# FFT convolution and spectral mixing on one core: a fourth PSUM slot for the transforms that run alone, and a later start of the first x loads

## The chip, the cores and the metric

The kernel runs on 1 core of a Trainium2 chip. The metric is the device time of one execution in microseconds (us); lower is better. Before the change it is 498.45 us, the median of 3 runs (497.08 to 500.85). PE is TensorE's matmul unit, DVE is VectorE, ACT is ScalarE, POOL is GpSimd; SP issues DMAs.

## The reference

Two layers over 8 sequences of 5696 steps and 128 channels, a long convolution and then a spectral mixing of 64 modes:

```python
def _attn_ref(x, h):                       # x (8, 5696, 128), h (5696, 128)
    Xf = np.fft.rfft(x, n=2 * S, axis=1)
    Hf = np.fft.rfft(h, n=2 * S, axis=0)
    return np.fft.irfft(Xf * Hf[None], n=2 * S, axis=1)[:, :S, :]

def _moe_ref(x, w_r, w_i, w_ch):           # w_r, w_i (64, 128, 128), w_ch (128, 128)
    X = np.fft.rfft(x, axis=1)
    Y = np.zeros_like(X)
    Xr, Xi = np.real(X[:, :64]), np.imag(X[:, :64])
    Y[:, :64] = (Xr @ w_r - Xi @ w_i) + 1j * (Xr @ w_i + Xi @ w_r)   # per mode
    u = x + np.fft.irfft(Y, n=S, axis=1)
    return u + np.maximum(u @ w_ch, 0.0)
```

## The kernel before, in words

**Transforms as matmuls.** The transform length 11392 is split as 89 x 128. A first transform (45 rows of a sequence against a small constant matrix) and a second one (a 128 x 128 constant per frequency, with the twiddles in it) make the spectrum. The second transform's constants are M: `m_sb[0]` is the real part, `m_sb[1]` the imaginary part, `m_sb[2]` the negative of the imaginary part, which DVE makes on the chip (L359). M is loaded in six pieces: three chunks of 15 frequencies each, for each chunk the real and then the imaginary part (L316 to L319).

**Stages.** They run in this order:

1. h, first transform: 16 tiles of 16 small matmuls (loop at L346, tile `Ah`), and then the three negations of M, one per chunk, on DVE.
2. h, second transform: 12 tiles of up to 16 matmuls (`h_tile`, from L368; reads `Ah` and M, writes `Hs`). Tiles 0 to 3 need M's first chunk, tiles 3 to 7 the second, tiles 7 to 11 the third.
3. x, first transform of the first pair of sequences: 32 tiles of 4 matmuls (`a_tile(j, True)`, L388; reads `Xin`, writes `As`). "Alone" means that nothing else is on PE meanwhile.
4. Four groups, each a pair of sequences: 27 ticks (`tick`, L409) do the second transform of two frequencies at a time, the product with `Hs` on DVE, a first inverse step that goes to a DRAM scratch, and the first 64 modes, which add up in PSUM bank 7 over the whole group. The next pair's first transform runs beside the last four ticks (16 tiles, 4 a tick) and then alone (16 tiles, L522). Ahead of those 16, `modes_out` (L476) copies bank 7 into `XM`; behind them, `modes_turn` (L479) transposes `XM` through bank 6.
5. Mixing of the modes, and the output stage (`u_tile`, `o_tile`).

**Slots.** PSUM has 8 banks. A tile takes two neighbouring banks, and `tile2` (L285) turns over three slots: banks 0-1, 2-3, 4-5. Banks 6 (`TB`) and 7 (`MB`) are kept for the modes. A matmul that starts a tile waits until the copy out of that slot's last tile is done. Those copies (`evac`, L264) alternate between ACT and DVE; in the alone tiles of x, 9 of 16 go to ACT and 7 to DVE (L331). The output stage has a counter of its own over four slots.

**Order.** Every engine executes its list in program order; a recorder (`R.add`) works out the semaphore waits from the tokens that are read and written. `after=` adds waits by hand. L281 is the line of the helper that records every matmul, L272, L274 and L275 those of the copies out of PSUM, L278 that of every DMA. DMAs are issued from two queues, each in program order:

- SP: small constants, then M's six pieces (they wait for h's first half), then the identity, `FQ`, `WV`, and, with the ticks, `Gs` (constants of the modes, three ticks ahead, seven of them in the first 40 us), the writes to scratch and the output.
- POOL: h in three pieces, then the first pair of x in six (two halves and a tail per sequence; L320; they wait for both halves of h), then `w_ch`, then the next pairs of x.

Of the kernel before, what the change touches and what calls it, by code (L numbers as in the profile page):

```python
# [4 lines left out]
P = 128  # L5
# [118 lines left out]
def bass_long_conv_fft__then__afno_spectral_mix_kernel(nc, x, h, moe_w_r, moe_w_i, moe_w_ch, out):  # L124
# [48 lines left out]
    def const(name, a):  # L173
        return nc.inline_tensor(np.ascontiguousarray(a.astype(np.float16)), name=name)

    KW = NQ * P
    c_m = const("cM", np.stack([mat.real, mat.imag], axis=1).reshape(P, -1))
# [15 lines left out]
    def at(name, cols, dt, off):  # L193
        return nc.alloc_sbuf_tensor_at(name, [P, cols], dt, offset=off)
# [9 lines left out]
    m_sb = [at(f"M{i}", KW, F16, a_m + i * KW * 2) for i in range(3)]  # L204
# [41 lines left out]
    def ap(t, row, p0, n, off, dims):  # L246
        return bass.AP(t, p0 * row + off, [[row, n]] + [list(d) for d in dims])
# [4 lines left out]
    def pv(bank, off, dims, p0=0, n=P):  # L252
        return bass.AP(ps, p0 * 4096 + bank * 512 + off, [[4096, n]] + [list(d) for d in dims])
# [5 lines left out]
    def bank(i):  # L259
        return ("bank", i)  # L260
# [16 lines left out]
    def dma(eng, dst, src, ring, reads=(), writes=(), after=()):  # L277
        return R.add(eng, lambda h_: h_.dma_start(dst, src), reads, writes, ring=ring, after=after)  # L278

    def mm(o, l, r, st, sp, reads, writes):  # L280
        return R.add("tensor", lambda h_: h_.matmul(o, l, r, start=st, stop=sp), reads, writes)  # L281

    slot3 = [0]

    def tile2():  # L285
        slot3[0] = (slot3[0] + 1) % 3
        return 2 * slot3[0]

    TB, MB = 6, 7

# [8 lines left out]
    def x_pieces(g_):  # L299
        for b in range(2):  # L300
            p0, off = b * NQ, x.offset + (2 * g_ + b) * S * D
            for c in range(2):
                yield (x_sb[p0:p0 + NQ - 1, c * half:(c + 1) * half],
                       bass.AP(x.tensor, off + c * half, [[P * D, NQ - 1], [1, half]]), ("xin", b, c))
            yield (x_sb[p0 + NQ - 1:p0 + NQ, 0:TAIL * D],
                   bass.AP(x.tensor, off + (NQ - 1) * P * D, [[TAIL * D, 1], [1, TAIL * D]]), ("xin", b, 2))

    h_loads = [dma("gpsimd", h_in[64 * c:64 * c + NQ - 1, :],
                   bass.AP(h.tensor, h.offset + c * half, [[P * D, NQ - 1], [1, half]]), "x", (), [("hin", c)])
               for c in range(2)]  # L310
# [2 lines left out]
                       "x", (), [("hin", 2)]))  # L313
    NCH = 3
    CH = NQ // NCH * P
    for c in range(NCH):  # L316
        for i in range(2):
            dma("sync", m_sb[i][:, c * CH:(c + 1) * CH], bass.AP(c_m, i * KW + c * CH, [[2 * KW, P], [1, CH]]), "c",
                (), [("m", i, c)], after=h_loads[:1])  # L319
    for dst, src, tok in x_pieces(0):  # L320
        dma("gpsimd", dst, src, "x", (), [tok], after=h_loads[:2])
    dma("sync", wi_sb[:, P:2 * P], c_i.ap(), "c", (), [("i16",)])
    dma("sync", fq_sb[:, :], c_fq.ap(), "c", (), [("fq",)])
    dma("sync", wv_sb[:, :], c_w.ap(), "c", (), [("wv",)])
# [4 lines left out]

    def a_tile(j, alone):  # L330
        eng = ("scalar" if 9 * j % 16 < 9 else "vector") if alone else None  # L331
        t = tile2()
        for i in range(4):
            mm(pv(t + i // 2, (i % 2) * 256, [[1, 256]]),
               ap(x_sb, P * D, 0, 2 * NQ, 4 * j + i, [[D, P]]), f1_sb[0:2 * NQ, :], True, True,
               XT_, [bank(t + i // 2)])
        evac(bass.AP(a_sb, 4 * j, [[2 * AW, P], [P, 180], [2, 2], [1, 2]]),
             pv(t, 0, [[1, 180], [512, 2], [256, 2]]),
             [bank(t), bank(t + 1)], [("as", j)], 1.0 / 64, eng)
# [3 lines left out]

    HT = [("hin", c) for c in range(3)] + [("hz",), ("fh",)]
    for j in range(16):
        t = tile2()  # L346
        for i in range(8):
            d = 8 * j + i
            for c in range(2):
                h_done = mm(pv(t + i // 4, (i % 4) * 90, [[1, 90]], 64 * c, 64),  # L350
                            ap(h_in, 64 * D, 64 * c, NQ, d, [[D, 64]]), fh_sb[64 * c:64 * c + NQ, :],
                            True, True, HT, [bank(t + i // 4)])
        evac(bass.AP(ah_sb, 8 * j, [[AW, P], [P, 90], [4, 2], [1, 4]]),
             pv(t, 0, [[1, 90], [512, 2], [90, 4]]),
             [bank(t), bank(t + 1)], [("ah", j)], 1.0 / 64)
    AHT = [("ah", j) for j in range(16)]
    for c in range(NCH):
        cs = slice(c * CH, (c + 1) * CH)
        R.add("vector", lambda e, cs=cs: e.tensor_scalar_mul(m_sb[2][:, cs], m_sb[1][:, cs], -1.0),  # L359
              [("m", 1, c)], [("m", 2, c)])  # L360

    def m_tok(k):
        return [("m", i, k * P // CH) for i in range(3)]

# [1 line left out]
    FORWARD = ((0, 0, 2), (1, 1, 0))  # L366

    def h_tile(j):  # L368
        t = tile2()
        ks = list(range(4 * j, min(4 * j + 4, NQ)))  # L370
        for i, k in enumerate(ks):
            b, o = t + i // 2, (i % 2) * 256
            re = bass.AP(ah_sb, (2 * k) * P, [[AW, P], [1, P]])
            im = bass.AP(ah_sb, (2 * k + 1) * P, [[AW, P], [1, P]])
            kc = slice(k * P, k * P + P)
            for half_, l0, l1 in FORWARD:
                o2 = o + half_ * P
                mm(pv(b, o2, [[1, P]]), m_sb[l0][:, kc], re, True, False, AHT + m_tok(k), [bank(b)])
                mm(pv(b, o2, [[1, P]]), m_sb[l1][:, kc], im, False, True, AHT + m_tok(k), [bank(b)])
        n = len(ks)  # L380
        evac(bass.AP(h_sb, 4 * j * P, [[2 * KW, P], [P, n], [KW, 2], [1, P]]),
             pv(t, 0, [[256, n], [P, 2], [1, P]]),
             [bank(t), bank(t + 1)], [("h", j)], 8.0)
# [119 lines left out]
    for g_ in range(NP):  # L503
        more = list(x_pieces(g_ + 1)) if g_ + 1 < NP else []
        todo_a = list(range(32)) if more else []
        for t in range(NT + LM):
            done = tick(g_, t)
            if t in X_AT and more:
                dst, src, tok = more.pop(0)
# [48 lines left out]
    m_done += [R.readers[tok][-1] for tok in HST]  # L558
    n_ev = [0]

    slot4 = [0]

    def tile4():
        slot4[0] = (slot4[0] + 1) % 4
        return 2 * slot4[0]

    def u_tile(i, b):
        g_, c = divmod(i, 8)
        t = tile4()
        for hb in range(2):  # L570
            o = pv(t + hb, 0, [[1, 360]])
            mm(o, c_sb[:, (2 * g_ + b) * P:(2 * g_ + b + 1) * P],
               ib_sb[:, (c * 16 + hb * 8) * NQ:(c * 16 + hb * 8 + 8) * NQ], True, False,
               [("c", g_ // 2), ("ib",)], [bank(t + hb)])
            for pl in range(8):
                o2 = (hb * 8 + pl) * 256 + b * P
                f0 = step * (c * 16 + hb * 8 + pl) % NA
                mm(pv(t + hb, pl * NQ, [[1, NQ]]), zt[i % NC][0:2 * NQ, o2:o2 + P], fq_sb[0:2 * NQ, f0:f0 + NQ],
                   False, pl == 7, [("zt", i % NC), ("fq",)], [bank(t + hb)])
        ub = (g_ % 2) * 2 + b  # L580
        n_ev[0] += 1
        evac(bass.AP(u_sb[ub], c * 16, [[KW, P], [P, NQ], [8, 2], [1, 8]]),
             pv(t, 0, [[1, NQ], [512, 2], [NQ, 8]]), [bank(t), bank(t + 1)],
             [("u", ub, c)], after=m_done, eng="scalar" if n_ev[0] % 8 in (0, 2, 3, 5, 7) else "vector")
# [3 lines left out]
    def o_tile(g_, b, r4):  # L588
        ub = (g_ % 2) * 2 + b
        bb = 2 * g_ + b  # L590
        t = tile4()
        i = n_o[0]
        n_o[0] += 1
        full = r4 < 11
        n, rows = (4, P) if full else (1, TAIL)
        rd = [("u", ub, c) for c in range(8)] + [("wch",), ("i16",)]
        for j in range(n):
            lh = bass.AP(u_sb[ub], 4 * r4 + j, [[KW, P], [44, P]]) if full else u_sb[ub][:, 44 * P:44 * P + TAIL]
            mm(pv(t + j // 2, (j % 2) * 256, [[1, 256]], 0, rows), lh, wi_sb[:, :], True, True, rd, [bank(t + j // 2)])
        bk = [bank(t), bank(t + 1)] if full else [bank(t)]  # L600
        rs, os_ = r_sb[i % NR], o_sb[i % NO]
        rv = bass.AP(rs, 0, [[512, rows], [P, n], [1, P]])
        ov = bass.AP(os_, 0, [[512, rows], [P, n], [1, P]])
        src_r, src_u = pv(t, 0, [[256, n], [1, P]], 0, rows), pv(t, P, [[256, n], [1, P]], 0, rows)
        R.add("scalar", lambda e: e.activation(rv, src_r, RELU), bk, [("r", i % NR)], after=[mixed])  # L605
        R.add("vector", lambda e: e.tensor_tensor(ov, src_u, rv, ADD), bk + [("r", i % NR)], [("o", i % NO)], after=[mixed])  # L606
        if full:
            dst = bass.AP(out.tensor, out.offset + bb * S * D + 4 * r4 * D, [[44 * D, P], [1, 4 * D]])
            src = o_sb[i % NO][:, :]
        else:  # L610
            dst = bass.AP(out.tensor, out.offset + bb * S * D + 44 * P * D, [[D, TAIL], [1, D]])
            src = o_sb[i % NO][0:TAIL, 0:P]
        dma("sync", dst, src, "o", [("o", i % NO)])
# [46 lines left out]
```

## Time and profile before

| | |
|---|---|
| time, median of 3 runs | 498.45 us |
| the profiled execution's own time | 496.65 us |
| its span, first to last instruction | 494.9 us |
| mean granted TensorE clock | 0.941 |
| PE busy | 422.2 us (85%) |
| DVE busy / ACT busy | 333.3 / 333.2 us (67% each) |
| h, first transform on PE | 16.5 to 31.5 us |
| h, second transform on PE | 33.3 to 50.7 us |
| x, first transform alone on PE | 51.0 to 71.5 us |
| the alone tiles of the next three pairs | from 133.2, 205.3 and 277.3 us, some 10 us each |

How to read it: times are from the span's start. A group "PE ps L281" is a matmul into PSUM. In the chain of work, each line is a start, a duration, and the work that the end of the program was waiting for then. In the lists of waits, the columns are the time waited in total, how often, and the longest. "PEclk" is the share of the full TensorE clock that was granted in a stretch.

### The profile page before, as it was taken

What the parts mean: (1) busy time and instruction counts of PE and PEld (TensorE: products, weight loads), DVE (VectorE), ACT (ScalarE), POOL (GpSimd) and SP (SyncE); (2) the same over time, 40 slices, a digit from 0 to 9 for tenths busy, and PEclk for the clock granted to TensorE, in tenths of its full rate; (3) what the DMA queues carried; (4) which work ended last, traced back from release to release, by engine and by line L of the source; (5) the groups of instructions that cost most, each with busy time, mean ns of one, the idle gap of its engine ahead of it and who ended that gap; (6) DMA issues with size and microseconds to landing.
All of it is one profiled execution on the core that took longest, in us unless ns stands there. A gap on an engine that the chain in (4) does not pass through costs nothing.

```text
span 494.9 us, 10143 instructions
## 1 busy us (share of the span) xinstructions
PE 422.2 (85%) x4188; PEld 333.7 (67%) x4188; DVE 333.3 (67%) x568; ACT 333.2 (67%) x416; POOL 41.2 (8%) x72
## 2 busy tenths in 40 slices
PE   0686998999989999979999979998598549597994
PEld 0686885777976777967777957776477427475873
DVE  0234759898669888869887679883137327465786
ACT  1233777988877988668988868984157426375795
POOL 1200000010100010100110010001031001010000
PEclk9998999999999999999999999999599858888998
DMA  8994008999909999919999369668789999999789
GB/s 129 282 169 118 1 0 141 250 235 250 191 19 155 264 259 227 180 21 188 272 222 251 89 158 274 183 164 228 239 213 257 282 309 360 313 350 320 293 296 341
DMA packets 97572, 105.05 MB, mean 212 GB/s; under 512 B 22924, under 2 KB 81692, under 8 KB 93724
## 3 DMA queue, kind: packets, MB, share of 16 engines
q1 hardware_dynamic: 75846, 63.47, 42.5%
q0 software_dynamic: 21680, 40.95, 41.2%
q8 instruction: 33, 0.54, 0.5%
q14 instruction: 13, 0.10, 0.1%
HBM read 74.82 MB, written 46.92 MB: 246 GB/s over the span
## 4 chain that ended last, share of the span: by engine, by line
PE 59%; DMA 25%; ACT 7%; DVE 6%; issue 1%; SPq 1%; DVEq 0%; ACTq 0%; POOLq 0%
PE ps L281 59%; DMA out_dram<-O 12%; DMA M<-cM 6%; DMA IBs<-cIB 4%; ACT R L605 3%; DMA zscr<-Zs 2%; DMA Hin<-in_h_dram 2%; ACT Xs L272 2%; DVE Pb L435 2%; DVE Xs L440 2%; DVE O L606 1%; DVE Xs L473 1%; ACT Zs L271 1%; ACT As L272 1%; SPq L278 1%
## 5 line engine op out<-in xcount | busy, mean ns | idle before, releaser
L272 ACT ACTIVATE Xs<-ps 128x1024 f16<-128x1024 f32 (+1 forms) x92 | 91.2, 1007 | 19.2 <-PE ps L281 19.2
L271 ACT CAST Zs<-ps 128x1024 f16<-128x1024 f32 (+1 forms) x92 | 93.4, 1017 | 12.5 <-PE ps L281 10.2
L281 PE MATMUL ps<-Xs,WV 128*128 128x512 f16 (+1 forms) x368 | 92.9, 375 | 7.7 <-DVE Xs L473 7.4
L281 PE MATMUL ps<-As,M 128*128 128x256 f16 x720 | 91.7, 273 | 3.4 <-ACT As L272 3.4
L606 DVE TENSOR_TENSOR O<-ps,R 128x512 f32<-128x512 f32 x96 | 59.3, 652 | 45.6 <-DMA out_dram<-O 27.9
L281 PE MATMUL ps<-F,Xin 90*128 90x256 f16 x512 | 80.1, 307 | 1.1 <-ACT Hs L272 0.3
L281 PEld LDWEIGHTS ps<-As,M 128*128 128x128 f16 x720 | 70.2, 98 | 12.9 <-DVE As L275 3.0
L435 DVE TENSOR_TENSOR Pb<-Xs,Hs 128x1024 f16<-128x1024 f16 (+1 forms) x92 | 62.4, 678 | 23.1 <-ACT Xs L272 22.9
L281 PEld LDWEIGHTS ps<-F,Xin 90*128 90x128 f16 x512 | 72.9, 232 | 7.4 <-DVE As L275 2.1
L473 DVE TENSOR_TENSOR Xs<-Xs,Pb 128x512 f16<-128x512 f16 (+1 forms) x184 | 77.3, 422 | 0.1
L275 DVE TENSOR_SCALAR As<-ps 128x720 f16<-128x720 f32 x59 | 58.8, 997 | 25.6 <-PE ps L281 24.8
L605 ACT ACTIVATE R<-ps 128x512 f32<-128x512 f32 x96 | 52.2, 573 | 32.7 <-PE ps L281 32.3
L272 ACT ACTIVATE As<-ps 128x720 f16<-128x720 f32 x69 | 60.8, 892 | 18.0 <-PE ps L281 17.9
L281 PE MATMUL ps<-WI,UT 128*128 128x256 f16 x360 | 58.6, 301 | 5.8 <-DVE O L606 5.6
L440 DVE TENSOR_TENSOR Xs<-Xs,Hs 128x1024 f16<-128x1024 f16 (+1 forms) x92 | 61.9, 672 | 0.1
L281 PE MATMUL ps<-IBs,C 128*128 128x360 f16 x128 | 44.7, 349 | 17.7 <-DVE O L606 16.5
L281 PEld LDWEIGHTS ps<-Xs,WV 128*128 128x128 f16 x368 | 35.0, 98 | 33.6 <-DVE Xs L473 10.9
L281 PE MATMUL ps<-Zs,Gs 128*128 128x256 f16 x360 | 54.3, 273 | 0.2 <-ACT Zs L271 0.2
L281 PEld LDWEIGHTS ps<-FQ,ZT 90*128 90x128 f16 x1024 | 45.0, 101 | 12.3 <-issue 3.5
L281 PE MATMUL ps<-FQ,ZT 90*128 90x45 f16 x1024 | 50.0, 189 | 1.6 <-issue 1.6
L281 PEld LDWEIGHTS ps<-Zs,Gs 128*128 128x128 f16 x360 | 35.0, 98 | 22.8 <-ACT Zs L271 1.6
L281 PEld LDWEIGHTS ps<-WI,UT 128*128 128x128 f16 x360 | 40.9, 154 | 12.5 <-DVE O L606 9.4
(41 smaller groups left out, 232.8 us busy)
## 6 DMA issues: line engine op xcount, KB each, us to landing
ZT<-zscr POOLq DMA_DIRECT2D x32, 720.0 KB, 10.3
zscr<-Zs SPq DMA_DIRECT2D x88, 256.0 KB, 5.9
out_dram<-O SPq DMA_DIRECT2D x88, 256.0 KB, 10.3
Gs<-cG SPq DMA_DIRECT2D x88, 128.0 KB, 5.8
Xin<-in_x_dram POOLq DMA_DIRECT2D x16, 704.0 KB, 8.3
M<-cM SPq DMA_DIRECT2D x6, 480.0 KB, 8.8
W<-in_moe_w_r_dram POOLq DMA_DIRECT2D x4, 512.0 KB, 10.2
W<-in_moe_w_i_dram POOLq DMA_DIRECT2D x4, 512.0 KB, 8.0
```

Source lines behind the costliest of these rows:

```text
L271: return R.add(e, lambda h_: h_.copy(dst, src), reads, writes, after=after)
L272: return R.add(e, lambda h_: h_.activation(dst, src, COPY, scale=scale), reads, writes, after=after)
L275: return R.add(e, lambda h_: h_.tensor_scalar_mul(dst, src, scale), reads, writes, after=after)
L278: return R.add(eng, lambda h_: h_.dma_start(dst, src), reads, writes, ring=ring, after=after)
L281: return R.add("tensor", lambda h_: h_.matmul(o, l, r, start=st, stop=sp), reads, writes)
L435: R.add("vector", lambda e: e.tensor_tensor(pbv, xv, hv[1], MULT), [tx] + HST, [tp], after=[h_done])
L440: R.add("vector", lambda e: e.tensor_tensor(xv, xv, hv[0], MULT), [tx], [tx])
L473: R.add("vector", lambda e: e.tensor_tensor(a, a, b, ADD if part else SUB), [("xs", s % NX), ("pb", s % NB_)], [("xs", s % NX), ("y", s % ...
L605: R.add("scalar", lambda e: e.activation(rv, src_r, RELU), bk, [("r", i % NR)], after=[mixed])
L606: R.add("vector", lambda e: e.tensor_tensor(ov, src_u, rv, ADD), bk + [("r", i % NR)], [("o", i % NO)], after=[mixed])
```

## The change

1. The counter of the slots takes their number. The first and second transforms of h and the alone tiles of x turn over four slots, banks 6 and 7 with them; tiles inside the ticks and beside them keep three. There is one counter now for all stages, the output stage too.
2. The first pair's x loads wait for h's second half and for the fourth piece of M (second chunk, imaginary part), where they waited for h's two halves.

```diff
-    slot3 = [0]
-
-    def tile2():
-        slot3[0] = (slot3[0] + 1) % 3
-        return 2 * slot3[0]
+    slot = [0]
+
+    def tile2(slots=3):
+        slot[0] = (slot[0] + 1) % slots
+        return 2 * slot[0]
...
+    m_loads = []
     for c in range(NCH):
         for i in range(2):
-            dma("sync", m_sb[i][:, c * CH:(c + 1) * CH], bass.AP(c_m, i * KW + c * CH, [[2 * KW, P], [1, CH]]), "c",
-                (), [("m", i, c)], after=h_loads[:1])
+            m_loads.append(dma("sync", m_sb[i][:, c * CH:(c + 1) * CH], bass.AP(c_m, i * KW + c * CH, [[2 * KW, P], [1, CH]]), "c",
+                (), [("m", i, c)], after=h_loads[:1]))
     for dst, src, tok in x_pieces(0):
-        dma("gpsimd", dst, src, "x", (), [tok], after=h_loads[:2])
+        dma("gpsimd", dst, src, "x", (), [tok], after=[h_loads[1], m_loads[3]])
...
     def a_tile(j, alone):
         eng = ("scalar" if 9 * j % 16 < 9 else "vector") if alone else None
-        t = tile2()
+        t = tile2(4 if alone else 3)
...
     for j in range(16):
-        t = tile2()
+        t = tile2(4)
...
     def h_tile(j):
-        t = tile2()
+        t = tile2(4)
...
-    slot4 = [0]
-
-    def tile4():
-        slot4[0] = (slot4[0] + 1) % 4
-        return 2 * slot4[0]
-
     def u_tile(i, b):
         g_, c = divmod(i, 8)
-        t = tile4()
+        t = tile2(4)
...
     def o_tile(g_, b, r4):
...
-        t = tile4()
+        t = tile2(4)
```

## The prediction

> **What bounds the kernel now**
>
> I read the page first, then the chain of work in order of time, then the waits and the timeline of its first 75 us, and last the timeline around the three later stretches of alone tiles.
>
> ```profile
> span 494.9 us, 10143 instructions
> ...
> PE   0686998999989999979999979998598549597994
> ...
> DMA  8994008999909999919999369668789999999789
> ...
> PE 59%; DMA 25%; ACT 7%; DVE 6%; issue 1%; SPq 1%; DVEq 0%; ACTq 0%; POOLq 0%
> ```
>
> One slice is 12.4 us. PE is the bound up to about 340 us, and time taken from PE's path there is taken from the end. Two stretches look soft: slices 2 to 4, where DMA is full too, and the stretches of alone tiles. The chain says what the first one is:
>
> ```profile
> 12.68 27.99 DMA M<-cM
> 40.69 0.66 DVE M L359
> 41.34 1.15 DVE Hs L275
> 42.54 8.07 PE ps L281 x112
> 50.62 1.38 ACT Hs L272
> 52.05 8.62 PE ps L281 x56
> ```
>
> The last piece of M, issued at 12.7, lands at 40.7; the negation waits for it; the copy of an `Hs` tile waits behind the negation on DVE; and PE waits for that tile's slot. The timeline shows the same from the engines' side (start, duration, engine, instructions, idle before):
>
> ```profile
> 33.27 5.42 PE L281 MATMUL ps<-Ah,M 128*128 128x128 f16 x64 [1.57 <-DVE M L359]
> ...
> 40.69 0.66 DVE L359 TENSOR_SCALAR M<-M 128x1920 f16<-128x1920 f16 x1 [6.90 <-DMA M<-cM]
> 41.26 2.35 DVE L275 TENSOR_SCALAR Hs<-ps 128x1024 f16<-128x1024 f32 x2
> 42.53 8.10 PEld L281 LDWEIGHTS ps<-Ah,M 128*128 128x128 f16 x116 [4.02 <-DVE Hs L275]
> 42.54 8.28 PE L281 MATMUL ps<-Ah,M 128*128 128x128 f16 x116 [3.85 <-DVE Hs L275]
> ```
>
> PE does 64 matmuls, four tiles, and stands still for 3.85 us. The clock pays again: the busy times by stretch have it at half speed in part of what follows (last columns: granted clock, DMA share, GB/s).
>
> ```profile
> 40.00:45.00 5.00, 2.46 (x33) 2.47 (x34) 2.92 (x3) 1.02 (x1) 0.00 (x0) 0.86 0.62 190
> 45.00:50.00 5.00, 5.00 (x75) 5.00 (x73) 2.72 (x3) 2.05 (x2) 0.00 (x0) 0.79 0.00 0
> ```
>
> In the matmuls' own records the starts are 107 ns apart from 33.3 to 36.8, 56 ns from there to the stall, 56 ns again for 1.1 us after it, 107 ns from 43.7 to 47.0, and 56 ns to the end of the stage at 50.65.
>
> **Why M is late.** The landing records give M's first four pieces at 17.1, 18.3, 19.5 and 20.75, one each 1.2 us, and the last two at 33.5 and 40.7. The x loads are issued from 16.58; their first packets move at 20.35, and then 16 KB packets of x (1.23 to 2.3 us each) share the engines with the rest of M. The last x lands at 42.3, the last of the `Gs` behind it at 45.3.
>
> **The alone tiles.** Undelayed, a tile of four matmuls takes PE 0.51 us (0.50 to 0.53, by the starts of those beside the ticks). In the alone stretch 30 tiles from 52.05 to 70.73 take 0.623 each: nearly every tile waits for its slot, and the first matmul of a waiting tile takes 0.24 us to the next, not 0.12 to 0.15. The copies meanwhile:
>
> ```profile
> 57.01 1.62 ACT L272 ACTIVATE As<-ps 128x720 f16<-128x720 f32 x2 [0.25 <-PE ps L281]
> 58.23 1.10 DVE L275 TENSOR_SCALAR As<-ps 128x720 f16<-128x720 f32 x1 [0.88 <-PE ps L281]
> 58.85 0.77 ACT L272 ACTIVATE As<-ps 128x720 f16<-128x720 f32 x1 [0.21 <-PE ps L281]
> ...
> 133.55 0.54 ACT L272 ACTIVATE XM<-ps 128x256 f16<-128x256 f32 x1
> ...
> 205.85 0.84 DVE L275 TENSOR_SCALAR XM<-ps 128x256 f16<-128x256 f32 x1
> ```
>
> (The last two are from the later stretches.) A copy takes 0.77 on ACT and 0.91 on DVE where it is undisturbed; where one of each overlaps, one of them takes 0.97 to 1.06 or 1.10 to 1.25. Both engines still wait for PE between copies, and PE for them: neither is full, so the three slots set the pace.
>
> **The change part by part**
>
> *x waits for M's fourth piece.* The wait ends at 20.75, not 16.5, so POOL issues x 4.2 us later. Behind x on POOL stands `w_ch` only, needed in the output stage; the next POOL instruction is at 75.9. SP's queue keeps its order. At 20.75 M has two pieces left, due at 21.9 and 23.1 at 1.2 us each. x's first packet follows its issue by 1.2 us (issue of 75.9) to 3.8 us (issue of 16.58), so comes at 22.0 to 24.5, when an engine has at most one piece's eight packets of M left. Before, the slowest engine needed 20.3 us for some 17 packets of M after x had come, 1.2 each; eight take at most 9.7, that is until 31.7. The third negation is due on DVE at 33.8, behind the `Ah` copies and two negations. Between 22 and 31.7 it makes no difference: the 6.9 us wait on DVE and the 3.85 on PE go. PE then runs through: 33 matmuls at 107 ns from 33.27 to 36.8, 147 at 56 ns, 8.2 us, end 45.0 instead of 50.65. The copies (ACT 1.02, DVE 1.23 for two tiles of 0.89) keep up. **Gain 5.65**, of it 3.85 the stall and most of the rest the half clock behind it. If the clock drops anyway, the gain is 3.85.
>
> *Is x there at 45.0?* It landed at 42.3 and starts 4.2 later: at worst 46.5. The other bound: an engine has 11 to 12 packets of x, 14.7 us at 1.23, from 22.0: 36.7, if nothing else moves. Between them: no transfer is added, and all of this traffic was done at 45.3; the engines have M to move until x comes, so x should not end after that. I take 42 to 44, and cost 0; bounds 0 and 1.5 (plus 1.7, half of a 3.4 us stretch at half clock, if the wait brings the clock down).
>
> *Four slots, h.* The first transform has PE at 107 ns a pair throughout, 0.89 per tile, against copies of 0.77 and 0.91 on alternate engines: no slot binds, 0. In the second one no slot binds once M is there, 0. At the entry to x, PE waits 0.36 us for DVE and 0.42 for ACT copies of `Hs` to free slots; a fourth slot covers both: **0.8**.
>
> *Four slots, the first 32 alone tiles.* With three, a slot's round (PE 0.66 to the end of the last matmul, start of the copy 0.04, copy 0.77 to 1.25, restart 0.06) is 1.5 to 2.0 us, 0.5 to 0.67 a tile, as seen. With four it is 0.38 to 0.5, below PE's 0.51. Next in line are the copies: of 16 tiles ACT has 9, at 0.81 to 1.03 with the turn, 0.46 to 0.58 a tile; DVE 7, at 0.95 to 1.18, 0.42 to 0.52. The pace lies between 0.51 (PE) and 0.62 (more overlap eats it all). I take 0.55, since PE's floor is 0.51 and overlapping copies, which will be the rule, put ACT above it: 30 x (0.623 - 0.55) = **2.2**, bounds 0 and 3.4.
>
> The Trainium skill, "PSUM — Partial Sum Buffer", Specifications (TRN2), says that ScalarE and VectorE read PSUM side by side at full bandwidth so long as they keep to different banks. These copies are in different banks and the rows above still stretch. By the page the pace would be PE's 0.51 and the sum 1.2 us better in these 32 tiles.
>
> *The later alone tiles, 3 x 16.* The same 0.07 a tile: 3.4. Against it a new wait: the fourth slot holds bank 7, which `modes_out` must have copied, and bank 6, which `modes_turn` needs. The counter, followed through the program, stands at 0 ahead of the ticks, so the fourth slot is the first alone tile of the first group, the second of the second, the third of the third. `XM` is copied by 134.09 and PE began that first tile at 133.15: 1.0 lost, with the other tiles and the next ticks behind it on PE. In the second group 206.69 against 205.98: 0.8. In the third 278.29 against 278.54: nothing. `modes_turn` waits at most for the last copy but one, while the next tick waits for the last: 0. Together 3.4 - 1.8 = **1.6**, bounds -1.8 and 3 x 16 x 0.11 - 1.8 = 3.5.
>
> The Trainium skill also has a case that speaks against this half of the change: in "TensorE: Matmul & The Clock Gate", HAM oscillation, a kernel that had been kept dense gained almost nothing from double-buffered PSUM (126.6 to 125.5 us). There the slots were not what PE waited for; here the 0.24 us first matmuls say that they are. By that case the sum would be 5.65 alone, less the new waits.
>
> *One counter.* The output stage begins on banks 4-5 instead of 2-3; its first tile needs the mixed modes either way: 0.
>
> *Sum.* 5.65 + 0.8 + 2.2 + 1.6 = 10.2 us. All of it lies ahead of 290 us, where PE is the chain; the tail moves as it stands. 496.65 - 10.2 = 486.4 for the profiled execution; the median of the runs shown is 1.8 above that execution, so 488.2.
>
> **The rivals**
>
> - *x becomes the wait.* x lands at up to 46.5 and PE stands still for 1.5, with 1.7 of half clock: 488.2 + 3.2 = 491.4. For it: x starts 4.2 later with a margin of 2.7. Against it: much of M is out of its way.
> - *The copies are the bound.* The pace stays at 0.62; 2.2 and 3.4 go: 493.8. For it: copies already stretch by 0.2 to 0.3 where they overlap. Against it: both engines wait for PE at 0.2 to 0.9 a time.
> - *M is late all the same,* behind x packets on one engine, past 38.5. A fifth tile is done ahead of the stall (16 x 0.056 = 0.9), and 5.65 shrinks to that: 492.9. Against it: eight packets are left at most.
> - *Slower: x lands so late that it eats everything.* The place is PE's first alone tile. The gains are gone when x lands at 45.0 + 10.2 = 55.2, and it is slower by over 1% from 60.2. That takes 12 packets from 24.5 at 3.0 us each; the slowest seen were 2.3 (then it lands at 52.1 and the time is 488.2 + 7.1 + 1.7 = 497.0).
>
> **How the numbers follow**
>
> My forecast has 0.68, x late 0.12, copies 0.11, M late 0.05, slower 0.04. The predicted time is the first's, 488.2. Its own range, with the bounds 0 and 3.4, -1.8 and 3.5, is 485 to 493; x late and most of the copies' case lie inside or just above. The range is 484.0 to 493.8: what is left out is the slower case, half of M late with more than one mishap, and a gain beyond all bounds, some 1.5 in 10. About 1%, 5.0 us, is what a measurement of this kernel can tell from no change, so faster means below 493.5: the forecast, x late, half of M late and a third of the copies' case, 0.85. Same 0.11, slower 0.04.
>
> **What would show it**
>
> M's last piece lands by 32 and DVE has no wait for it; the second transform of h runs from 33.3 to 45 without a pause and without a drop of the clock after 36.8; the last x lands before 45 (if not, PE shows a wait for a DMA of `Xin`); the alone tiles come at 0.55 and end on PE at about 62.5, not 71.5; PE waits 1.0 for the copy of `XM` on ACT in the first group and 0.8 for that on DVE in the second. The prediction is wrong if the third negation still waits, if x lands after 46.5, or if the alone tiles keep 0.62.

## The result and the profile after

The changed kernel takes 483.39 us (median of 4 runs, 481.19 to 484.3) against 498.84 (497.08 to 500.85): 15.4 us less, a ratio of 0.9683 with a 95% interval of 0.9633 to 0.9733. The forecast was faster, 488.2, in a range of 484.0 to 493.8. The direction held and both halves of the change paid, but the gain that was forecast, 10.2 us, was too small by a third, and the time lies 0.6 us below the range. The profiled execution took 481.19, with a span of 479.4; that of before 496.65 and 494.9, so the two profiles stand to each other as the medians do. One run of experiment 3 below (497.02 us) was in a slower state, and its median is given without it.

The page after; the rows are those shown of before, slices of 12.0 us:

```profile
span 479.4 us, 10143 instructions
...
PE   0689979999979999989999989996899369597994
...
DMA  7994049999749999769899298759699999999779
...
PE 56%; DMA 26%; ACT 7%; DVE 7%; issue 1%; POOL 1%; SPq 0%; DVEq 0%; ACTq 0%; POOLq 0%
```

The chain of work in its first 65 us (start, duration, what):

```profile
11.94 8.92 DMA M<-cM
21.14 2.51 POOL Xin L278 x5
23.65 21.39 DMA Xin<-in_x_dram
45.13 16.64 PE ps L281 x128
61.79 0.78 ACT As L272
62.62 1.06 PE ps L281 x8
```

The 28 us of M are gone from it. A transfer of x stands in their place, which ends at 45.0; then 128 matmuls follow each other without a wait, where before they were cut into pieces of 4 to 56. The timeline of the same stretch (start, duration, engine, instructions, idle before):

```profile
31.79 1.79 DVE L360 TENSOR_SCALAR M<-M 128x1920 f16<-128x1920 f16 x3
...
32.50 11.52 PE L281 MATMUL ps<-Ah,M 128*128 128x128 f16 x180 [1.58 <-DVE M L360]
...
45.13 16.63 PE L281 MATMUL ps<-F,Xin 90*128 90x256 f16 x128 [1.10 <-DMA Xin<-in_x_dram]
```

The three negations stand in a row, PE does all 180 matmuls of h's second transform in one run, and the first alone tile waits 1.1 us for x. In the landing records M's six pieces come at 17.2, 18.4, 19.6, 20.9, 22.1 and 23.4. Busy time by stretch (the last three columns are the granted clock, the DMA share and GB/s):

```profile
35.00:40.00 5.00, 5.00 (x90) 5.00 (x88) 3.08 (x3) 2.50 (x3) 0.00 (x0) 1.00 0.91 193
40.00:45.00 5.00, 4.02 (x73) 3.85 (x69) 3.38 (x4) 3.07 (x3) 0.00 (x0) 1.00 0.32 58
45.00:50.00 5.00, 4.87 (x38) 4.90 (x39) 3.23 (x4) 3.47 (x5) 0.00 (x0) 1.00 0.02 3
```

No second stretch at half clock. Where the 15.5 us of span came from, by the starts on PE in both profiles:

| stretch | before | after | gain | forecast |
|---|---|---|---|---|
| start to the first alone tile | 51.01 | 45.13 | 5.9 | 6.0 |
| first alone tile to the first tick | 21.36 | 17.49 | 3.9 | 2.6 |
| first group (ticks, then 16 alone tiles) | 71.81 | 70.64 | 1.2 | 1.6 for the three groups |
| second group | 72.24 | 70.82 | 1.4 | (see above) |
| third group | 71.96 | 70.26 | 1.7 | (see above) |
| last group's first tick to the end | 206.48 | 205.03 | 1.45 | 0 |

### The profile page after: what moved, and what is told of

Its sections match the earlier page's. It is cut to its first block, busy times and chain, and to the rows that moved or that the text cites. A ratio compares the mean times of both kernels' runs of the same rounds, so it can differ in the third digit from the quotient of the medians.

```text
span 479.4 us, 10143 instructions
## 1 busy us (share of the span) xinstructions
PE 411.6 (86%) x4188; PEld 326.9 (68%) x4188; DVE 329.9 (69%) x568; ACT 330.1 (69%) x416; POOL 41.5 (9%) x72
## 3 DMA queue, kind: packets, MB, share of 16 engines
q0 software_dynamic: 21680, 40.95, 42.3%
## 4 chain that ended last, share of the span: by engine, by line
PE 56%; DMA 26%; ACT 7%; DVE 7%; issue 1%; POOL 1%; SPq 0%; DVEq 0%; ACTq 0%; POOLq 0%
PE ps L281 56%; DMA out_dram<-O 12%; DMA Xin<-in_x_dram 4%; DMA IBs<-cIB 4%; ACT R L600 3%; DMA Hin<-in_h_dram 2%; DMA M<-cM 2%; DMA zscr<-Zs 2%; ACT Xs L272 2%; DVE Pb L436 2%; DVE Xs L441 2%; DVE O L601 2%; ACT Zs L271 1%; DVE Xs L474 1%; ACT As L272 1%
## 5 line engine op out<-in xcount | busy, mean ns | idle before, releaser
L281 PE MATMUL ps<-F,Xin 90*128 90x256 f16 x512 | 71.7, 295 | 2.2 <-DMA Xin<-in_x_dram 1.1
L281 PEld LDWEIGHTS ps<-F,Xin 90*128 90x128 f16 x512 | 68.2, 225 | 4.9 <-ACT Hs L272 1.2
L275 DVE TENSOR_SCALAR As<-ps 128x720 f16<-128x720 f32 x59 | 56.2, 952 | 21.8 <-PE ps L281 19.3
L272 ACT ACTIVATE As<-ps 128x720 f16<-128x720 f32 x69 | 57.3, 843 | 13.9 <-PE ps L281 12.6
## 6 DMA issues: line engine op xcount, KB each, us to landing
out_dram<-O SPq DMA_DIRECT2D x88, 256.0 KB, 10.2
```

What stands on the lines that cost most here:

```text
L272: return R.add(e, lambda h_: h_.activation(dst, src, COPY, scale=scale), reads, writes, after=after)
L275: return R.add(e, lambda h_: h_.tensor_scalar_mul(dst, src, scale), reads, writes, after=after)
```

## The experiments

Ratios are to the kernel before on the same chip; times are medians, of four runs or more where nothing else is said. The changed kernel's own 483.4 us is the one given above, not taken again beside each experiment, and the medians of the kernel before lie at 498.05 to 498.84 from one comparison to the next. So a difference between two variants is read from the stretches of their profiles as well. A line "..." marks code that is left out. "Pace" is the mean distance from one alone tile's start on PE to the next, over 30 of the first 32 tiles.

**1. The slots alone.** x waits as before:

```diff
-        dma("gpsimd", dst, src, "x", (), [tok], after=[h_loads[1], m_loads[3]])
+        dma("gpsimd", dst, src, "x", (), [tok], after=h_loads[:2])
```

> Only the slots are changed; the first x loads wait for the two halves of h, as before. Theory: the two halves of the change add up. The last piece of M still lands near 41 us, PE does five tiles of the second transform of h instead of four ahead of the stall (0.9 us), the entry to x saves 0.8, the first 32 alone tiles run at 0.51 us each instead of 0.62 (3.4) and the later ones save 4.3 together: 498.8 - 9.4 = about 489.4 us. Rival, the fourth slot hides M's lateness by itself: then the second transform of h ends near 45 us and the time is that of the whole change, about 484.

487.98 us, ratio 0.980 (0.9752 to 0.9849). The chain has M back:

```profile
13.27 29.32 DMA M<-cM
42.59 0.02 issue
42.61 0.66 DVE M L360
43.27 1.14 DVE Hs L275
44.41 0.05 issue
44.46 7.92 PE ps L281 x96
```

96 matmuls after the stall, not 112: five tiles were done ahead of it, as expected, and that is all a fourth slot does for M's lateness. In this execution M landed 1.9 us later still and 6.8 us ran at half clock, so h ended at 52.4. The alone tiles ran at 0.532 us (the third starts 0.92 after the second, since it waits for a copy of `Hs`) and the three groups took 4.6 less than before. The theory holds; the rival would have had h end near 45.

**2. The x loads alone.** x as in the change, three slots in the transforms:

```diff
     def a_tile(j, alone):
...
-        t = tile2(4 if alone else 3)
+        t = tile2(3)
...
     for j in range(16):
-        t = tile2(4)
+        t = tile2(3)
...
     def h_tile(j):
-        t = tile2(4)
+        t = tile2(3)
```

> Only the x loads are changed (they wait for the fourth piece of M); all transforms keep three slots. Theory: the stall in the second transform of h goes, PE comes to the first alone tile at about 45 us instead of 51 and waits there about 1 us for x; the alone tiles stay at 0.62 us each, and nothing changes later: 498.8 - 5.9 = about 493 us. Rival, without the fourth slot the earlier M brings nothing, since three slots then bind in the second transform of h: about 498.

490.39 us, ratio 0.9832 (0.9777 to 0.9886); the theory's 493 is a little high, the rival's 498 is out. In the profile PE comes to the first alone tile at 45.73 us, 5.3 earlier than before; of the stretches behind it only the last is shorter (204.16 us for 206.48), and experiment 11 shows that one to scatter as much. From the chain:

```profile
32.67 12.64 PE ps L281 x176
45.31 0.02 issue
45.34 1.36 ACT Hs L272
46.70 0.05 issue
46.74 7.46 PE ps L281 x48
54.21 0.02 issue
54.23 1.14 DVE As L275
```

Three slots are enough for h's second transform once M is there. The entry to x costs a wait for a copy of `Hs` again, and the alone tiles, cut into pieces again, go at 0.623.

**3. Three slots for the first 32 alone tiles.**

```diff
...
     for j in range(32):
-        a_tile(j, True)
+        a_tile(j, True, 3)
```

(The third argument, here and in experiments 4 and 7, is the number of slots.)

> The changed kernel, but the first 32 alone tiles turn over three slots. Theory: the pace of the alone tiles is set by the slots, so these 32 go back to 0.62 us each: 483.4 + 3.4 = about 487 us. Rival, the pace came from something else (fewer transfers in that stretch, a warmer PE): it stays at 0.51 and the time at 483.4.

485.51 us (three runs, 485.03 to 487.75), ratio 0.9756 (0.97 to 0.9812): 2.1 above the changed kernel by the medians. The stretch that was changed, from the first alone tile to the first tick, takes 20.88 us for 17.49: 3.4 more, as in the theory. The pace is 0.622, and the copies are long again. Groups of that stretch (count, busy, mean ns, idle before them), first of this kernel:

```profile
L281 PE MATMUL ps<-F,Xin 90*128 90x256 f16 x128 | 19.9, 309 | 0.6 <-DMA Xin<-in_x_dram 0.6
...
L272 ACT ACTIVATE As<-ps 128x720 f16<-128x720 f32 x18 | 15.7, 892 | 4.6 <-PE ps L281 4.6
L275 DVE TENSOR_SCALAR As<-ps 128x720 f16<-128x720 f32 x14 | 14.2, 1016 | 6.4 <-PE ps L281 6.2
```

and then of the changed kernel:

```profile
L281 PE MATMUL ps<-F,Xin 90*128 90x256 f16 x128 | 16.6, 292 | 1.1 <-DMA Xin<-in_x_dram 1.1
...
L272 ACT ACTIVATE As<-ps 128x720 f16<-128x720 f32 x18 | 14.4, 818 | 3.3 <-PE ps L281 2.8
L275 DVE TENSOR_SCALAR As<-ps 128x720 f16<-128x720 f32 x14 | 13.1, 939 | 4.6 <-PE ps L281 3.8
```

With four slots the copies are more crowded in time and yet shorter, and both engines still wait for PE.

**4. Three slots for the later alone tiles.**

```diff
...
         while todo_a:
-            a_tile(todo_a.pop(0), True)
+            a_tile(todo_a.pop(0), True, 3)
```

> The changed kernel, but the alone tiles of the second, third and fourth pair turn over three slots. Theory: these 3 x 16 tiles give back 1.2 + 1.4 + 1.7 us, and the waits for the copy of the modes go with them: 483.4 + 4.3 = about 487.7 us. Rival, the gain between the groups came from the ticks (another order of the slots): about 483.4.

487.95 us, ratio 0.9788 (0.9733 to 0.9842): 4.6 above the changed kernel, theory 4.3. The groups take 71.65, 72.42 and 72.38 us, as before the change and 4.7 more in all than in the changed kernel, and their alone tiles come at 0.62. The rival, the ticks, is out.

**5. x after M's third piece.**

```diff
-        dma("gpsimd", dst, src, "x", (), [tok], after=[h_loads[1], m_loads[3]])
+        dma("gpsimd", dst, src, "x", (), [tok], after=[h_loads[1], m_loads[2]])
```

> The changed kernel, but x waits for M's third piece, not its fourth. Theory: x is what PE waits for at its first alone tile (1.1 us in the changed kernel); x is issued 1.2 us earlier and lands 1.2 earlier, near 43.8 us, M still lands whole by 25, and the time falls by 1.1 to about 482.3. Rival, the gate can't come earlier: packets of x then cut in among M's last two pieces, the third negation waits again (past 34 us), and the time rises by up to 5 us.

481.47 us, ratio 0.9674 (0.9615 to 0.9733), not to be told from the changed kernel by the time. The wait for x is gone: PE's waits between 30 and 75 us (total, times, longest) are

```profile
PE ps L281 <- DVE Xs L474: 1.8, 1, 1.8
PE ps L281 <- DVE M L360: 1.6, 1, 1.6
PE ps L281 <- ACT As L272: 0.9, 1, 0.9
PE ps L281 <- ACT Hs L272: 0.2, 1, 0.2
```

x landed at 44.1 and M at 23.7, so the rival's interleaving did not come. But h's second transform ended later (45.1 for 43.8), since the clock stayed at half until 37.5 us in this execution and until 35.3 in that of the change: the 1.1 us were won and lost to the phase of the clock. And not all of them were to be had: with x out of the way, the third alone tile waits for the last full copy of `Hs` (0.97 us behind the second; 0.92 in experiment 1 and 0.82 in experiment 9, which don't wait for x either), and the stretch from the first alone tile to the first tick takes 18.01 us for 17.49.

**6. x after M's last piece.** `m_loads[5]` in the same place, a single run.

> The changed kernel, but x waits for M's sixth and last piece. Theory: x is issued 2.4 us later, lands near 47.5 us, PE's wait for it grows from 1.1 to about 3.6 us, and the first tick starts 2.5 us later than in the changed kernel (62.6 there); if such a gap brings the clock down, 1.7 us more. Rival, the transfers have slack and x ends where it ended (45): no difference.

483.26 us. x was issued at 23.8, 2.65 us later than in the changed kernel, and landed at 45.6, only 0.6 later; the first tick started at 63.2, 0.6 later. The theory's 47.5 is wrong and the rival is nearer; PE waited 0.9 us, not 3.6, and a copy of `Hs` that it needed ended at 45.66, as late as x. x landed at 42.3, 44.1, 45.0 and 45.6 for issues at 16.6, 20.3, 21.1 and 23.8: a later x catches up about half of its delay (3.9 of 7.2 us from the first to the last). That less of M and of the small loads stands in its way then is the likely reason, and not shown.

**7. The modes' slot later.** The first three alone tiles behind the ticks keep three slots:

```diff
...
         while todo_a:
-            a_tile(todo_a.pop(0), True)
+            a_tile(todo_a.pop(0), True, 3 if len(todo_a) >= 13 else 4)
```

> The changed kernel, but of the 16 alone tiles behind the ticks the first three keep three slots, so that the slot with the modes' banks comes up at the fourth or fifth tile. Theory: the waits of PE for the copy of the modes (0.7 us above the pace in the first group, 0.3 in the second) go: 1.0 us less, about 482.4, with no start-to-start of 1.2 or 0.85 among these tiles. Rival, the pause only lets the copies catch up, and they bind a little later: no difference.

481.55 us, ratio 0.9681 (0.9606 to 0.9756). In the changed kernel PE waits for the copy of the modes in the middle of the first alone tile: its first two matmuls go to bank 6, the third to bank 7, at 124.16.

```profile
121.82 1.90 PE L281 MATMUL ps<-F,Xin 90*128 90x256 f16 x12
...
123.71 0.39 ACT L272 ACTIVATE XM<-ps 128x256 f16<-128x256 f32 x1
...
124.16 3.09 PE L281 MATMUL ps<-F,Xin 90*128 90x256 f16 x22 [0.44 <-ACT XM L272]
```

In this one it runs through:

```profile
121.75 5.47 PE L281 MATMUL ps<-F,Xin 90*128 90x256 f16 x38
...
123.91 0.51 ACT L272 ACTIVATE XM<-ps 128x256 f16<-128x256 f32 x1
```

The start-to-starts of 1.23 and 0.85 are gone, but the three groups together are only 0.1 us shorter (70.36, 70.76 and 70.49 against 70.64, 70.82 and 70.26). By the starts, the first three steps of the three stretches are 0.5 us shorter in all, since steps of 0.6 take the place of the long ones; the third group, which had no such wait, is 0.2 longer, which is within its scatter (71.24 in experiment 6 with the same tiles). The wait was real, and taking it away was worth 0.1 to 0.5 us, not 1.0.

**8. Copies on one engine at a time,** three slots, a single run (the third argument is here the engine that copies):

```diff
...
-        t = tile2(4 if alone else 3)
+        t = tile2(3)
...
     for j in range(32):
-        a_tile(j, True)
+        a_tile(j, True, "scalar" if j < 16 else "vector")
```

> The changed kernel with three slots everywhere for the alone tiles, and in the first 32 of them the copies of tiles 0 to 15 are all on ACT and those of 16 to 31 all on DVE. Theory of the prediction: a copy is stretched by a copy of the other engine that runs at the same time, so with one engine at a time every ACT copy takes 0.77 us and every DVE copy 0.91. Rival: the stretch belongs to something else (PE's writes into the neighbouring slot), and copies of 0.97 and more are still there. Either way these tiles are slower than with both engines, 0.8 to 0.95 us each.

496.45 us. The copies on ACT still alternate, even tiles 0.86 to 0.90, odd ones 0.77; on DVE 0.98 to 1.00 and 0.88. So a long copy does not need the other engine, and the prediction's reading of it is wrong. The long ones are shorter here than the 0.97 and 1.10 upward with both engines, but that goes with the clock, which was at half: experiment 11, at half clock with both engines, has the same 0.88 to 0.90 and 0.99 to 1.01. The pace was 0.85, for a reason not expected (see the last section).

**9. Both mends** (5 and 7 together).

> The changed kernel with two mends: x waits for M's third piece, and the first three alone tiles behind the ticks keep three slots. Theory: both small waits go (1.1 us for x, 1.0 for the copies of the modes), so 483.4 - 2.1 = about 481.3, and about 1 us below either mend alone (481.5 each). Rival, what is saved ahead of the ticks is lost to the pace of the output stage: 483.4 as the changed kernel.

482.5 us, ratio 0.968 (0.964 to 0.972): not to be told from the changed kernel, nor from either mend. PE reaches the first alone tile at 44.56 instead of 45.13, and the first tick at 62.48 instead of 62.62; the rest of the 0.57 goes to the wait for `Hs` that experiment 5 has. The mends are worth some tenths of a microsecond together.

**10. Even tiles first,** three slots, a single run (the third argument is here the place in the order, by which the engine is chosen):

```diff
...
-    for j in range(32):
-        a_tile(j, True)
+    for n, j in enumerate(list(range(0, 32, 2)) + list(range(1, 32, 2))):
+        a_tile(j, True, n)
```

> The changed kernel, but the first 32 alone tiles turn over three slots and are done in another order: the 16 with even numbers first, then the 16 with odd numbers (each engine copies at the same places in the order). Theory: the long copies (0.97 us and more on ACT, 1.10 and more on DVE) belong to the even tiles, that is to where in As they write; then the first 16 copies are long and the last 16 short (0.77 and 0.91). Rival: every second copy is long by its place in the order: then they still alternate.

483.86 us. Neither theory nor rival: no copy is long at all.

```profile
L272 ACT ACTIVATE As<-ps 128x720 f16<-128x720 f32 x18 | 13.6, 770 | 6.6 <-PE ps L281 6.6
L275 DVE TENSOR_SCALAR As<-ps 128x720 f16<-128x720 f32 x14 | 12.7, 908 | 7.3 <-PE ps L281 7.3
```

Both engines copy at the same time here as in experiment 3, and the means are 770 and 908 ns for 892 and 1016. What differs is that no tile is followed by its neighbour: tile j writes 8 bytes at 8j in each row of 256 bytes, so an even tile and the odd one behind it fill one aligned block of 16. PE reads `Xin` for tile j in the same pieces, 8 bytes at 8j in each row of 256, so the order of its reads changed with that of the writes. The pace falls from 0.622 to 0.578 with the same three slots.

**11. Before, again,** a single run for a second profile.

> The kernel before, once more, for a second profile of it. Theory: the stages up to the output stage repeat to within 0.5 us and the output stage scatters by some us, so that a difference of 1.5 us there means nothing. Rival: the output stage repeats too (206.5 us from the first tick of the last group to the end).

The theory did not hold. This execution took 510.65 us with the clock at half from 56.8 to 87.6, so its earlier stages are compared with nothing here. Its last stretch, from the last group's first tick to the end, took 205.2 where the first profile has 206.5; over the other kernels, whose code is the same there but for the slot that it starts with, that stretch runs from 203.5 to 207.4. So the table's 1.45 us in that row is within the scatter.

## Why the prediction was right and wrong

- *M and the stall: right.* M is whole at 23.4 (bound: 31.7; its "some 17 packets" of M on the slowest engine no record shows, and on average 6.4 an engine were left to start when x came), the stall and the second half clock are gone, and PE comes to the first alone tile 5.9 us earlier (forecast 6.0). The end of h is 1.2 earlier than forecast: 0.8 because its second transform could start that much earlier (0.53 of it is a pause in the first transform of h that the profile before has and this one hasn't), 0.4 from the clock's phase (half clock ends at 35.3, not 36.8).
- *x at no cost: wrong by 1.1 us.* I took 42 to 44 and it landed at 45.0, inside the bounds. The argument that all of this traffic had been done at 45.3, and would be again, was the better one: I drew less from it than it says. That PE was 1.2 early hid the miss in the sum, which was luck.
- *Fourth slot in h: right in place, too dear.* Only the entry to x gains by it (experiment 2), but not 0.8: where PE doesn't wait for x there, the fourth alone tile starts 2.06 to 2.22 us after the last matmul of h (experiments 1, 5 and 9) for 2.58 before, 0.4 to 0.5 less. In the changed kernel the wait for x covers it.
- *The alone tiles' pace: the step that failed.* I priced 0.55, "since PE's floor is 0.51 and overlapping copies, which will be the rule, put ACT above it". It is 0.512: PE's floor. The step took the long copies for something that two engines do to each other, and so for the rule once the slots no longer bind. They were real, but one engine alone has them (experiment 8) and two engines side by side needn't (experiment 10). With four slots, ACT's mean is 0.818, nine of 16 tiles at that and a turn of 0.04 make 0.48 a tile, below PE. The 0.04 a tile is 1.2 us in the first 32 tiles and 1.9 in the later 48.
- *The page weighed against it.* The Trainium skill, "PSUM — Partial Sum Buffer", Specifications (TRN2), has ScalarE and VectorE read different banks at full bandwidth side by side. Experiment 10 agrees: 770 and 908 ns with both engines at work. I let the row overrule the page, where the row had another cause.
- *The case against four slots,* from "TensorE: Matmul & The Clock Gate", does not carry over: experiments 3 and 4 price the slots at 3.4 and 4.7 us by the stretches of their profiles.
- *The new waits for the modes' banks: right in place, too dear.* They are in the first alone tile of the first group and the second of the second, as the counter said; by the starts of the tiles 0.7 and 0.3 us are lost instead of 1.0 and 0.8. I had the whole tile wait, but half of it goes to bank 6 and went ahead. Taking them out gave 0.1 to 0.5 (experiment 7).
- *The output stage: 0 forecast, 1.45 in the profile.* One execution each; the scatter of that stretch covers it. It stays open whether any of it belongs to the change.

The sum: 10.2 forecast; 1.2 and 1.9 for the pace, 0.8 for the waits, and 1.45 of the output stage make some 15.5. The range failed by 0.6: its low end was the sum with every bound at its best (13.4) and 1 us more. The alone tiles came in at their bounds or past them (4.3 in the later ones, bound 3.5, since the waits were dearer in the bound than on the chip), and the last stretch was given no scatter.

## What to carry to other kernels

When a ring of buffers sets the pace, price the next size at the floor of the engine that waits, and doubt any number for the other engines that was taken while the ring was tight. A load that the next stage doesn't need yet is best kept behind one that it does: holding back x by itself brought PE to the first alone tile 5.3 us earlier (7.9 us by the medians), and x, issued 4.6 us later, landed 2.8 later. When one wait is taken out, look for what ends just behind it: here it was a copy of `Hs`. Before a stretched duration is put down to contention, ask which instructions are stretched: here it was every even tile, and the order of the tiles, not the number of engines, was behind it.

## What the runs showed of the hardware

**Long copies.** Undisturbed, the copy of an alone tile into `As` takes 771 ns (ACT) or 908 (DVE). That of an even tile takes 0.85 to 1.27 us where its odd neighbour, the other half of the same aligned 16 bytes, follows it. That holds with one engine (experiment 8) and vanishes when neighbours are 16 tiles apart (experiment 10). The neighbour's copy is not the cause by itself: in experiment 5 tiles 0 and 1 are copied at the same time, PE is done with both, and neither copy is long.

```profile
45.12 1.35 PE L281 MATMUL ps<-F,Xin 90*128 90x256 f16 x8
46.49 0.77 ACT L272 ACTIVATE As<-ps 128x720 f16<-128x720 f32 x1
46.50 0.91 DVE L275 TENSOR_SCALAR As<-ps 128x720 f16<-128x720 f32 x1 [0.41 <-PE ps L281]
```

The records tie the length to PE's work on the neighbour: of 640 long copies in these profiles (experiments 8 and 11, with their half clock, left aside) 617 end 0.35 to 0.42 us (ACT) or 0.45 to 0.54 (DVE) after PE's last matmul of the neighbour, whenever the neighbour's own copy starts. The copies of 57 even tiles that are of normal length though the neighbour follows all start when that matmul has begun, or at most 0.12 us before. Whether PE's reads of `Xin`, in the same 16-byte blocks of its rows, are behind it, and how, no run shows.

**A clock that stays down under a busy PE.** In experiment 8 the clock was at half from 47.5 to 78.2 us, with PE busy without a gap up to 72.7 (duration, then PE, PEld, DVE, ACT, POOL busy; clock, DMA share, GB/s):

```profile
50.00:55.00 5.00, 5.00 (x26) 4.82 (x25) 0.00 (x0) 4.75 (x7) 0.00 (x0) 0.50 0.02 3
55.00:60.00 5.00, 5.00 (x25) 4.86 (x24) 0.07 (x1) 4.68 (x6) 0.00 (x0) 0.50 0.00 0
60.00:65.00 5.00, 5.00 (x25) 4.88 (x24) 5.00 (x6) 0.00 (x0) 0.00 (x0) 0.50 0.00 0
```

A tile of four matmuls of 256 columns then takes 0.85 us, which is eight times the 107 ns of 128 columns, and PE, not the copies, is the bound. These tiles did not release the clock in 25 us, while with the 128 x 128 matmuls of h it is released within 2.8 to 5.5 us. Experiment 11 has the same in the kernel before, between 56.8 and 87.6. Of the profiles in which the later alone tiles have three slots, three of five show a drop of the clock or more after the first tick had begun (experiments 2, 4 and 11); of the eight with four slots, none does until PE waits for the output stage's constants (`IBs`), as it does in all of them. That more waits bring the clock nearer to a drop fits this and is not proven by it.

**The phase of the clock.** Half clock at the start of h's second transform lasted 2.8 to 5.5 us from one execution to the next (experiment 2 has the longest), which moves its end by up to 1.3 us. That is read from the matmuls' starts, 107 ns apart and then 56; the rows by stretch print 1.00 there, since the first clock record of an execution is the one that ends this half clock. Differences of a microsecond in one profile are not to be trusted here.
